# A linear-attention and tanh-shrink kernel on one core: the last tile's output in two transfers instead of four, and one middle tile's in four instead of two

## The chip, the cores and the metric

The kernel runs on one core of one Trainium2 chip. The metric is the device time of one execution in microseconds (us); lower is better. The core has five engines: TensorE (PE) for matrix products, VectorE (DVE), ScalarE (ACT), GpSimd (POOL) and SyncE (SP), which here only begins transfers. The transfers themselves are carried by the core's 16 DMA engines.

## The reference

`q`, `k` and `v` have the shape (8, 8, 576, 64): batch, heads, sequence, head size. The first part is linear attention with phi(x) = elu(x) + 1, the second a layer of two matrix products with x - tanh(x) between them.

```python
def phi(x):
    return np.where(x > 0, x, np.exp(x) - 1.0) + 1.0
q_p, k_p = (phi(q), phi(k))
kv = np.einsum('bhsd,bhse->bhde', k_p, v)
z = np.sum(k_p, axis=2)
num = np.einsum('bhsd,bhde->bhse', q_p, kv)
den = np.einsum('bhsd,bhd->bhs', q_p, z)[..., None] + 1e-06
attn_out = num / den
...
x = attn_out.transpose(0, 2, 1, 3).reshape(B * S, H * D)   # 4608 x 512
h = x @ w_in                                               # 512 -> 2048
g = h - np.tanh(h)
out = g @ w_out                                            # 2048 -> 512, float32
```

## The kernel before, in words

**Tiling.** The 4608 tokens are taken in nine chunks (`NC = 9`, loop over `c` at line 557) of 512. The attention of each of the eight batches is computed piecemeal between the matrix products of the chunks before it; its result lands transposed in `xT`. For a chunk, the first layer runs over 16 blocks of 128 hidden columns (line 654 on): four accumulating products (`l1mm`, line 413) a block, then ScalarE's tanh and VectorE's subtraction into `gT` (`l1act2`, line 417). The second layer (line 673 on) runs over four tiles `i` of 128 tokens, each a sum of 16 products of 128 x 512 (`l2mm`, line 433). The order of all work on the engines is the order in which the program is written; small tables (`s1`, `s2`) say after which block or step which piece of the next batches' attention is done.

**Tokens and rows.** Within a batch, a token is numbered s = 9 p + j, with p from 0 to 63 and j from 0 to 8 (`J = 9`). A chunk's columns are ordered by j first and p second, so a tile of 128 tokens is two groups of 64: partitions 0 to 63 hold one j, partitions 64 to 127 the next. Two neighbouring partitions of a group are nine output rows apart. The last tile of the program (chunk 8, tile 3) holds j = 7 and j = 8 of the last batch.

**How a tile leaves.** `evac` (line 438) is called once for a finished tile. It takes a new `osb` buffer (128 x 512 float32, one of five), copies the tile's columns `f0` to `f1` out of the accumulator, on ScalarE or, if `f0` is not 0, on VectorE, and begins the transfers to `out`. There is one transfer for each of the tile's two groups of 64 partitions (`half`), of 64 rows of 2048 bytes. In chunk 3, the transfers of tiles 0 and 1 are cut at column 256, so that there are four of 64 rows of 1024 bytes to a tile (`cuts`, line 449). All of these are begun by SyncE, with one exception below.

**The last tile** (line 678 on) is summed in two parts, columns 0 to 383 and then columns 384 to 511, with 16 products each, and `evac` is called for each part: first with `f0 = 0`, `f1 = 384`, copied by ScalarE, then with `f0 = 384`, `f1 = 512`, copied by VectorE. For this tile (`last`, line 446) the first group of 64 partitions is sent by SyncE and the second by ScalarE (line 451). After that only the program's closing is left: SyncE waits for the transfers that are still under way, and the engines meet at a barrier.

**Counts.** 78 transfers go to `out` in all: 66 of 128 KB, 8 of 64 KB, and, for the last tile, two of 96 KB and two of 32 KB.

Of the kernel before, what the change touches and what calls it, by code (L numbers as in the profile page):

```python
# [18 lines left out]
def kernel(  # L19
# [9 lines left out]
    nc = tc.nc  # L29
    B, H, S, D = q.shape  # L30
# [5 lines left out]
    NC = N // 512  # L36
    J = S // 64
# [400 lines left out]
    def evac(c, i, o, f0=0, f1=None):  # L438
        f1 = DM if f1 is None else f1
        osb = opool.tile([128, DM], F32, name="osb")  # L440
        if f0:
            nc.vector.tensor_copy(osb[:, f0:f1], o[:, f0:f1])  # L442
        else:
            nc.scalar.copy(osb[:, f0:f1], o[:, f0:f1])  # L444

        last = c == NC - 1 and i == 3
        for half in range(2):
            b, j = divmod(2 * (4 * c + i) + half, J)
            cuts = [f0, 256, f1] if c == 3 and 2 * i + half < 4 else [f0, f1]
            for a0, a1 in zip(cuts, cuts[1:]):  # L450
                (nc.scalar if last and half else nc.sync).dma_start(
                    out=out[b * S:(b + 1) * S, a0:a1].rearrange("(p j) m -> p j m", j=J)[:, j, :],
                    in_=osb[64 * half:64 * half + 64, a0:a1])

# [17 lines left out]
    for n in range(2):  # L472

        nc.gpsimd.dma_start(out=w_out_sb[:, 8 + 2 * n:10 + 2 * n, :],
                            in_=moe_w_out[1024 + 256 * n:1280 + 256 * n, :].rearrange("(ko ki) f -> ki ko f", ki=128))
# [3 lines left out]
    for h in range(2):  # L479
        for hg in range(2):  # L480
            for i in range(2):
                m = 4 * hg + 2 * h + i
# [74 lines left out]
    for c in range(NC):  # L557
# [44 lines left out]
        elif n1 < B:  # L602
# [11 lines left out]
            m = 12 if c == 1 else 9  # L614
# [58 lines left out]
        for s in range(16):  # L673

            (g, i) = divmod(s, 4) if c == 0 else (s % 4, s // 4)
            if g == 0:
                os_[i] = ps_all[:, i if c == 0 else 4 + i % 2, :]
            if c == NC - 1 and i == 3:

                if g == 0:  # L680
                    o2 = ps_all[:, 0, :]
                    for o, f in ((os_[i], slice(0, 384)), (o2, slice(384, DM))):
                        for fi in range(NF):
                            nc.tensor.matmul(o[:, f], gT[:, fi, 384:512], w_out_sb[:, fi, f],  # L684
                                             start=(fi == 0), stop=(fi == NF - 1))
                        evac(c, i, o, f.start, f.stop)
                continue
            if c == 0 and g == 2:
                for n in (2 * i, 2 * i + 1):
                    f = 8 + 2 * (n // 4)  # L690
                    l2mm(gT, os_[n % 4], n % 4, f, f + 2)
            else:
                l2mm(gT, os_[i], i, 4 * g, 4 * g + 4)
            if g == 3:
                evac(c, i, os_[i])
            for f in s2[s]:
                f()
# [30 lines left out]
```

## Time and profile before

| | |
|---|---|
| median of 3 runs | 286.83 us (286.57 to 286.95) |
| the profiled execution, its own time | 286.75 us |
| its span, first to last instruction | 285.0 us |
| mean granted TensorE clock | 0.997 |
| end of the last product (L684) | 280.84 us |
| ScalarE's copy of the last tile's 384 columns (L444) | 279.97, 0.48 us |
| VectorE's copy of its 128 columns (L442) | 280.86, 0.29 us |
| transfers to `out` begun by SyncE at L451 | 76, each 0.47 to 1.05 us of SyncE, median 0.59 |
| transfers to `out` begun by ScalarE at L451 | 2, of 0.56 and 0.68 us |

The span is the time from the first to the last instruction of the profiled execution; the difference to its own time lies ahead of and behind the program. Times within the profile count from the span's start. PE is TensorE, with PEld its weight loads; "SPq" and "ACTq" are the sequencers of SyncE and ScalarE, which issue transfers; "q1" and "q10" are the DMA queues of SyncE's and of ScalarE's transfers, "q0" that of GpSimd's. A transfer is made of packets, here one for each contiguous row, and of small packets of 4 bytes that tell of its completion. "us to landing" counts from the issue to the last of these. The DMA share of a window is the mean busy share of the 16 DMA engines; where packets of one engine overlap in the records it can exceed 1.

### The profile page before, as it was taken

To read this page: it belongs to the slowest core of one execution; us is meant where nothing else is said; L and a number is where in the kernel's file an instruction comes from. 1 tells how busy PE (TensorE), PEld (TensorE's weight loads), DVE (VectorE), ACT (ScalarE), POOL (GpSimd) and SP (SyncE) were. 2 spreads that over 40 slices of the span, in tenths; PEclk is the share of its full clock that TensorE was granted. 3 is DMA by queue.
4 is the path that set the end of the run, shared out by engine and by line. 5 is a ranking of instruction groups with operands and counts; after the bars stand their busy time and mean duration, and the time that the engine had idled before them with its cause. 6 is when DMAs were issued, how large, how long until landed. Compare 5 with 4: busy or idle time off the path is not lost.

```text
span 285.0 us, 5076 instructions
## 1 busy us (share of the span) xinstructions
PE 278.0 (98%) x2085; PEld 130.7 (46%) x2085; DVE 174.1 (61%) x271; ACT 147.4 (52%) x182; POOL 74.2 (26%) x66
## 2 busy tenths in 40 slices
PE   8989999999999999999999999999999999999994
PEld 3544454444444454445444544444444444444442
DVE  3759967997479773877397639764870166007500
ACT  4848557847345663666366635573642364135410
POOL 8642030030260536143604360506050000000000
PEclk9999999999999999999999999999999999999998
DMA  6999999998992399038903692232014200330033
GB/s 100 195 206 213 207 207 208 230 169 160 227 234 56 71 195 219 1 85 150 239 9 83 105 236 62 68 89 56 20 45 112 58 17 2 74 74 0 2 74 75
DMA packets 38215, 32.99 MB, mean 116 GB/s; under 512 B 16016, under 2 KB 33840, under 8 KB 38064
## 3 DMA queue, kind: packets, MB, share of 16 engines
q0 software_dynamic: 17488, 18.35, 39.7%
q1 hardware_dynamic: 20544, 14.18, 20.1%
q8 instruction: 16, 0.26, 0.4%
q10 hardware_dynamic: 160, 0.13, 0.2%
q14 instruction: 7, 0.06, 0.0%
HBM read 38.01 MB, written 9.46 MB: 167 GB/s over the span
## 4 chain that ended last, share of the span: by engine, by line
PE 85%; DMA 11%; POOL 2%; issue 0%; DVE 0%; POOLq 0%
PE ps_all L435 40%; PE ps_all L414 39%; DMA v<-in_v_dram 8%; DMA w_in_sb<-in_moe_w_in_dram 3%; PE ps_all L179 2%; PE ps_all L267 1%; PE ps_all L684 1%; POOL kraw L88 1%; POOL v L88 0%; POOL qraw L88 0%; POOL v L469 0%; PE ps_all L275 0%; POOL qraw L91 0%; PE ps_all L326 0%; PE ps_all L161 0%
## 5 line engine op out<-in xcount | busy, mean ns | idle before, releaser
L414 PE MATMUL ps_all<-xT,w_in_sb 128*128 128x512 bf16 x574 | 125.7, 379 | 0.0
L435 PE MATMUL ps_all<-w_out_sb,gT 128*128 128x512 bf16 x560 | 124.6, 379 | 0.0
L421 DVE TENSOR_TENSOR gT<-ps_all,th 128x1024 bf16<-128x1024 f32 x64 | 77.8, 1218 | 47.0 <-ACT th L420 47.0
L420 ACT ACTIVATE th<-ps_all 128x1024 f32<-128x1024 f32 x64 | 65.5, 1023 | 47.7 <-PE ps_all L414 47.7
L414 PEld LDWEIGHTS <-w_in_sb 128*128 128x128 bf16 x574 | 55.9, 98 | 67.3
L435 PEld LDWEIGHTS <-gT 128*128 128x128 bf16 x560 | 53.8, 98 | 63.3 <-issue 0.2
L444 ACT COPY osb<-ps_all 128x512 f32<-128x512 f32 (+1 forms) x36 | 20.8, 582 | 56.3 <-PE ps_all L435 40.0
L238 POOL TENSOR_TENSOR qp<-qp,rd 128x1152 bf16<-128x1152 bf16 x10 | 21.0, 2117 | 39.1 <-issue 23.6
L224 POOL TENSOR_TENSOR pr<-qp,zb 128x1152 f32<-128x1152 bf16 x10 | 23.5, 2361 | 24.0 <-ACT zb L217 21.6
L131 ACT ACTIVATE e<-qraw 128x1152 bf16<-128x1152 bf16 x16 | 18.5, 1160 | 8.9 <-DMA qraw<-in_q_dram 8.9
L229 DVE TENSOR_REDUCE dn<-pr 128x9 f32<-128x576 f32 x20 | 14.5, 746 | 12.2 <-POOL pr L224 12.2
L131 ACT ACTIVATE e<-kraw 128x1152 bf16<-128x1152 bf16 x15 | 17.4, 1162 | 0.1
L133 DVE TENSOR_TENSOR qp<-e,r 128x1152 bf16<-128x1152 bf16 x16 | 12.1, 759 | 5.5 <-ACT e L131 4.6
L133 DVE TENSOR_TENSOR kp<-e,r 128x1152 bf16<-128x1152 bf16 x15 | 11.4, 759 | 5.5 <-ACT e L131 4.6
L91 POOL DMA_DIRECT2D kraw<-in_k_dram x7 | 5.6, 803 | 28.1 <-ACT e L131 19.8
L426 DVE TENSOR_TENSOR gT<-ps_all,th 128x512 bf16<-128x512 f32 x16 | 10.3, 686 | 2.4 <-ACT th L425 1.7
L425 ACT ACTIVATE th<-ps_all 128x512 f32<-128x512 f32 x16 | 9.2, 598 | 4.6 <-PE ps_all L414 3.4
L91 POOL DMA_DIRECT2D qraw<-in_q_dram x7 | 5.2, 744 | 23.5 <-DVE r L132 13.0
L497 PE MATMUL ps_all<-zero 128*128 128x512 bf16 x29 | 9.5, 491 | 1.2 <-DVE zero L456 1.2
L374 DVE CAST xT<-ps_all 128x1024 bf16<-128x1024 f32 x5 | 6.1, 1217 | 6.9 <-PE ps_all L275 6.9
L132 DVE TENSOR_SCALAR r<-qraw 128x1152 bf16<-128x1152 bf16 x16 | 7.5, 467 | 3.2 <-DMA qraw<-in_q_dram 3.2
L442 DVE COPY osb<-ps_all 128x128 f32<-128x128 f32 x1 | 0.3, 292 | 11.6 <-PE ps_all L684 11.6
(96 smaller groups left out, 132.4 us busy)
## 6 DMA issues: line engine op xcount, KB each, us to landing
out_dram<-osb SPq DMA_DIRECT2D x66, 128.0 KB, 2.4
kraw<-in_k_dram POOLq DMA_DIRECT2D x7, 576.0 KB, 6.8
qraw<-in_q_dram POOLq DMA_DIRECT2D x7, 576.0 KB, 8.8
v<-in_v_dram POOLq DMA_DIRECT2D x7, 576.0 KB, 12.0
w_in_sb<-in_moe_w_in_dram POOLq DMA_DIRECT2D x3, 512.0 KB, 13.0
w_out_sb<-in_moe_w_out_dram POOLq DMA_DIRECT2D x3, 512.0 KB, 18.8
rdb<-ds SPq DMA_DIRECT2D x2, 576.0 KB, 7.9
qraw<-in_q_dram POOLq DMA_DIRECT2D x2, 288.0 KB, 4.5
```

Of the source, the lines that this page charges most:

```text
L91: nc.gpsimd.dma_start(out=t.rearrange("q h i j d -> q (h i) (j d)"), in_=x.rearrange("(n q) x -> q n x", n=4))
L131: return (lambda: nc.scalar.activation(e, x, AF.Exp), lambda: nc.vector.tensor_scalar(r, x, 0.0, 1.0, ALU.max, ALU.add), lambda: nc.vector ...
L133: lambda: nc.vector.tensor_tensor(y, e, r, ALU.min))
L224: nc.gpsimd.tensor_mul(pr_t[b][:, i].rearrange("p j h d -> p j (h d)"), qp_t[b][:, i].rearrange("p j h d -> p j (h d)"), zb_t[b][:, i].uns ...
L229: nc.vector.tensor_reduce(dn_t[b][:, i, :, h], pr_t[b][:, i, :, h, :], mybir.AxisListType.X, ALU.add)
L238: nc.gpsimd.tensor_mul(x, x, rd[:, i].unsqueeze(2).to_broadcast([128, J * 2, D]))
L414: nc.tensor.matmul(h, w_in_sb[:, p, fi * 128:(fi + 1) * 128], xT[:, p, c * 512:(c + 1) * 512], start=(n == 0), stop=(n == NP - 1))
L420: nc.scalar.activation(th, h, AF.Tanh)
L421: nc.vector.tensor_sub(gT[:, fi:fi + 2, :], h, th)
L426: nc.vector.tensor_sub(gT[:, fi, :], h, th)
L435: nc.tensor.matmul(o, gT[:, fi, i * 128:(i + 1) * 128], w_out_sb[:, fi, :], start=(fi == 0), stop=(fi == NF - 1))
L444: nc.scalar.copy(osb[:, f0:f1], o[:, f0:f1])
```

## The change

The last tile no longer goes through the loop over its two groups of 64 partitions. Each of the two calls of `evac` for it begins one transfer, from SyncE, of all 128 partitions: 128 rows of 1536 bytes (192 KB) for the first call and 128 rows of 512 bytes (64 KB) for the second. The destination is written as a pattern of three dimensions, j (2 values) by p (64) by columns; the source is the `osb` buffer's 128 partitions by columns. ScalarE begins no transfers any more.

In chunk 3, tile 2 is now cut at column 256 too: it leaves in four transfers of 64 rows of 1024 bytes instead of two of 2048. (The old condition `2 * i + half < 4` held for tiles 0 and 1.) The number of transfers to `out` stays 78.

```diff
-        last = c == NC - 1 and i == 3
+        if c == NC - 1 and i == 3:
+            nc.sync.dma_start(
+                out=out[(B - 1) * S:, f0:f1].rearrange("(p j) m -> j p m", j=J)[J - 2:J],
+                in_=osb[:, f0:f1])
+            return
         for half in range(2):
             b, j = divmod(2 * (4 * c + i) + half, J)
-            cuts = [f0, 256, f1] if c == 3 and 2 * i + half < 4 else [f0, f1]
+            cuts = [f0, 256, f1] if c == 3 and i < 3 else [f0, f1]
             for a0, a1 in zip(cuts, cuts[1:]):
-                (nc.scalar if last and half else nc.sync).dma_start(
+                nc.sync.dma_start(
                     out=out[b * S:(b + 1) * S, a0:a1].rearrange("(p j) m -> p j m", j=J)[:, j, :],
                     in_=osb[64 * half:64 * half + 64, a0:a1])
```

## The prediction

> **What bounds the kernel now.** I read the page first, then the chain of waits over the end of the span, then the end engine by engine, then the transfers there, since the diff touches only what follows the last results and one pair of transfers in the middle.
>
> ```profile
> span 285.0 us, 5076 instructions
> PE 278.0 (98%) x2085; PEld 130.7 (46%) x2085; DVE 174.1 (61%) x271; ACT 147.4 (52%) x182; POOL 74.2 (26%) x66
> ```
>
> TensorE is busy for 278.0 of 285.0 us, so the body is its own time, and a transfer counts only where TensorE waits for it or where nothing but the transfer is left. The chain of waits from 262 us on shows where the second begins:
>
> ```profile
> 266.97 10.36 PE ps_all L435 x48
> 277.33 3.51 PE ps_all L684 x32
> 280.84 0.02 issue
> 280.86 0.29 DVE osb L442
> ```
>
> The chain's last piece of work is VectorE's copy of 128 columns, done at 281.15. From there to 285.0 lie 3.85 us in which no engine computes: the output leaves and the program closes. Everything the diff does to the last tile falls here, in the open. The end in order of time:
>
> ```profile
> 279.97 0.48 ACT L444 COPY osb<-ps_all 128x384 f32<-128x384 f32 x1 [2.01 <-DMA out_dram<-osb]
> 280.48 1.18 SPq L451 DMA_DIRECT2D out_dram<-osb  x2
> 280.48 1.39 ACTq L451 DMA_DIRECT2D out_dram<-osb  x2
> ```
>
> ScalarE's copy of 384 columns ends at 280.45; SyncE and ScalarE then each begin a transfer of 64 rows of 1536 bytes at 280.48, and one of 64 rows of 512 bytes at about 281.19, as soon as the VectorE copy is done. What the DMA engines did meanwhile (columns: window, length, five engines, clock, DMA share, GB/s):
>
> ```profile
> 281.50:281.60 0.10, 0.00 (x0) 0.00 (x0) 0.00 (x0) 0.00 (x0) 0.00 (x0) 1.00 0.05 15
> ...
> 281.90:282.00 0.10, 0.00 (x0) 0.00 (x0) 0.00 (x0) 0.00 (x0) 0.00 (x0) 1.00 1.00 200
> ...
> 282.20:282.30 0.10, 0.00 (x0) 0.00 (x0) 0.00 (x0) 0.00 (x0) 0.00 (x0) 1.00 1.16 384
> ...
> 282.90:283.00 0.10, 0.00 (x0) 0.00 (x0) 0.00 (x0) 0.00 (x0) 0.00 (x0) 1.00 0.08 5
> ```
>
> First bytes move just before 281.6, 1.1 us after the issue; all 16 engines are full by 281.7; the bulk is over by 282.9 and a few late packets end at 283.2. The last landing is ScalarE's 32 KB transfer:
>
> ```profile
> out_dram<-osb SPq DMA_DIRECT2D x1, 96.0 KB, 2.1
> out_dram<-osb ACTq DMA_DIRECT2D x1, 32.0 KB, 2.8
> ```
>
> 281.19 + 2.8 = 284.0. From that landing to the span's end is 1.0 us of closing, which the change does not touch. The profiled execution took 286.75 us, so 1.75 us lie outside its span; it is 0.08 below the median of 286.83.
>
> **The change, part by part.**
>
> Mid transfers. The third tile of chunk 3 leaves in four transfers of 1024-byte rows instead of two of 2048. SyncE begins them at 136.08. Four issues at about 0.6 us (the issue row's median is 0.59) keep it until 138.5; its next transfer cannot begin before the next tile's copy is done:
>
> ```profile
> 139.03 0.59 ACT L444 COPY osb<-ps_all 128x512 f32<-128x512 f32 x1 [2.71 <-PE ps_all L435]
> ```
>
> That is 139.62, 1.1 us later, and behind it SyncE has nothing until the transpose at 153.2. The four run beside the loads for the coming chunk; the v load, issued at 133.22 with 10.1 us to landing, is there at 143.3, and no engine takes up that chunk's inputs before ScalarE's exponential at 153.77. Bytes stay the same. Cost taken: 0, hidden by those 10 us; without that cover it would be the two added issues, 1.2 us. Below nothing it can't go, since TensorE is full in every microsecond from 126 to 146.
>
> Removed at the end. ScalarE's two issues (0.56 and 0.68 us) and SyncE's two of 64 rows. ScalarE has no work behind them, so this frees nothing by itself.
>
> Added at the end. Two SyncE issues of 128 rows. Eight-row issues took 0.29 us, 64-row ones 0.47, so by the line through them 128 rows take 0.67: 280.48 to 281.15, just when the 128 columns are ready. If an issue took 1.0 us instead, the second would begin at 281.5, and its rows, as the next step shows, have to wait far longer than that anyway. Cost: 0.
>
> How many DMA engines carry them. Here lies the whole sum. The old destination was 64 rows by columns. The new one is written "j p m": its outermost count is 2 (the two row residues j), then 64, then the columns; the source stays 128 partitions. No transfer of this trace has an outermost count of 2. The nearest rows: the 32 KB and 96 KB transfers of ScalarE's queue (64 rows outermost), and four of 8 rows at 66.5 to 68.3 (L355), alone in their queue (first line: transfers by queue from 281.4 to 283.4; second: from 66.5 to 68.3; packets, MB, share):
>
> ```profile
> q10 hardware_dynamic: 160, 0.13, 22.0%
> ...
> q1 hardware_dynamic: 64, 0.02, 6.8%
> ```
>
> Of 160 packets, 128 are rows, leaving 32 completion packets of 4 bytes, 16 a transfer, which I read as one for each engine. Of 64, 32 are rows, leaving 32, so 8 a transfer: eight rows outermost, eight engines. Bounds: 2 engines, if the outermost count goes on setting it, and 16, if the 128 rows are shared out like the 64. An outermost count of 2 is nearer to 8 than to 64, so I take 2.
>
> The Trainium skill, page "DMA: Bandwidth & Descriptors", section "Why a DMA increments its semaphore by 16 and not by 1", states that the engines used are the largest number up to 16 that divides both sides' slowest dimension; 2 and 128 give 2. Its section "Rules for kernel authors" speaks for the change in one line (two transfers of partition halves only serialize, use one of 128 partitions) and against it in another (an outermost size below 16 confines the transfer to that many engines). The eight-row transfers here, on 8 engines, agree with the rule; a 2 beside a 128 no run here shows yet. By the rule the sum is that of 2 engines, by the line on partition halves alone it would be that of the 16-engine rival below.
>
> Time on 2 engines. Each carries 64 rows of 1536 bytes, then 64 of 512, one after the other, since both transfers stand in SyncE's queue. The packet records of the end give 65 ns (median in ScalarE's transfer) to 111 (in SyncE's, where 16 engines pulled at 64 partitions) for 1536 bytes, and 27 to 34 ns for 512. With two engines moving instead of 16 I expect less crowding, so I take 65 and, between 27 and 34, 30: 64 x 65 = 4.16 us, 64 x 30 = 1.92 us, together 6.1. As a cross-check, 384 GB/s over 16 engines is 24 GB/s each, and 131,072 bytes at that rate are 5.5 us. Lower bound: consecutive packets in that burst start 53 and 23 ns apart, 64 x 76 = 4.9 us. Upper: 111 and 34, 9.3 us.
>
> The sum: first bytes 281.6, + 6.1 = 287.7; + 0.4 from last packet to landing (SyncE's 96 KB: last packet at 282.2, landed at 282.6); + 1.0 closing = 289.1 us of span, where it was 285.0; + 1.75 = 290.8 us. Bounds: 289.6 with 4.9, 294.0 with 9.3. Where the stall goes: SyncE's closing waits stand on these two transfers, and nothing else is late.
>
> **The rivals.**
>
> *Sixteen engines all the same* (the other side). If the shape is shared out over 16 engines, eight rows each, the wide part moves as it does now, and the narrow part, begun at 281.19, ends at 282.9 without ScalarE's copy of the traffic; landed 283.3 instead of 284.0, it saves 0.7 us at best and nothing if the late packets up to 283.2 remain: 286.3 us. For it speaks that the 64-row transfers, the closest in size, post 16 completions; against it the 8-row ones. The deciding point: 128 rows over e engines at 65 + 30 ns are 12.2/e us, against 1.6 us now (281.6 to 283.2): from 8 engines up it is not slower.
>
> *Two engines, each packet paying its own latency.* In the records the last four 512-byte packets of the present run, following an 8 KB instruction fetch on one engine, start some 60 ns apart, though nothing else moves. At 60 for the narrow and 111 for the wide rows: 7.1 + 3.8 = 10.9 us, 295.6 us. Against it: narrow packets elsewhere in the same 2 us follow each other at 23 ns.
>
> *The mid transfers cost something.* It needs the loads late by more than 10 us; it would add at most 1.2 us to either case. I give it no chance of its own.
>
> **How the numbers follow.** Two engines at ordinary packet times: 0.83. Two engines, slower still: 0.08. Sixteen engines: 0.09, of which 0.06 is faster by over 0.2% (0.6 us, about what a measurement of this kernel can tell from no change) and 0.03 within it. Time: the likeliest case's 290.8 us. Range: that case's bounds, 289.6 to 294.0; what it leaves out is 0.17 plus a little noise. Faster 0.06, same 0.03, slower 0.91.
>
> **What would show it.** Right: the page's queue 10 is gone or empty; in the last stretch DMA share sits near 2/16 = 0.12 and about 45 GB/s for some 6 us; the 192 KB transfer takes 5 to 6 us from issue to landing and the 64 KB one 6 to 7; the chain up to VectorE's copy still ends near 281.15. The completion packets of the two transfers number 4, not 32. Wrong: share near 1 after 281.6 (16 engines), or a copy that ends later than 281.3, which would put the cost into the middle.

## The result and the profile after

The changed kernel takes 291.07 us (291.0 to 291.6, 5 runs) against 286.58 us (286.37 to 286.95, 5 runs) for the kernel before: a ratio of 1.0158, interval 1.0146 to 1.0171. It is 4.5 us slower. The forecast was 290.8 us, range 289.6 to 294.0.

The profiled execution is the slowest of the five, 291.6 us, with a span of 289.7. The chain of waits reaches VectorE's last copy almost as early as before, and SyncE begins both transfers without delay (chain of the span's end, then SyncE's timeline: start, length, what):

```profile
281.10 0.29 DVE osb L442
```

```profile
280.71 1.23 SPq L447 DMA_DIRECT2D out_dram<-osb  x2
```

The copy ends at 281.39 instead of 281.15: the body was 0.24 us longer in this execution, and the whole rest of the 4.7 us of span lies behind it. The same stretch that was 3.8 us long (281.15 to 285.0) is 8.3 us long (281.39 to 289.7). What the DMA engines do in it (window, length, five engines, clock, DMA share, GB/s):

```profile
281.90:284.50 2.60, 0.00 (x0) 0.00 (x0) 0.00 (x0) 0.00 (x0) 0.00 (x0) 0.83 0.14 33
284.50:286.90 2.40, 0.00 (x0) 0.00 (x0) 0.00 (x0) 0.00 (x0) 0.00 (x0) 0.50 0.13 50
286.90:288.40 1.50, 0.00 (x0) 0.00 (x0) 0.00 (x0) 0.00 (x0) 0.00 (x0) 0.50 0.14 43
288.40:289.70 1.30, 0.00 (x0) 0.00 (x0) 0.00 (x0) 0.00 (x0) 0.00 (x0) 0.50 0.00 0
```

A share of 0.13 to 0.14 of 16 engines is two engines, busy for 6.5 us, where before all 16 were full for one. 50 GB/s is 25 for each of the two in the wide rows, 43 is 21.5 in the narrow ones; the first 2.6 us bring only 33. The clock column falls to 0.50 only in this end, 2.6 us after TensorE's last product (281.06); up to there it is 1.0. The longer end at 0.50, not a slower body, makes the span's mean clock 0.990, where it was 0.997. The transfers by queue, over the same end:

```profile
q1 hardware_dynamic: 260, 0.26, 11.9%
```

260 packets are 256 rows and 4 completions, two for each transfer, where the old four transfers had 64. ScalarE's queue q10 is no longer in the page.

### The profile page after: what moved, and what is told of

Read it like the earlier page. It is cut to its first block, busy times and chain, and to the rows that moved or that the text cites. A ratio compares the mean times of both kernels' runs of the same rounds, so it can differ in the third digit from the quotient of the medians.

```text
span 289.7 us, 5047 instructions
## 1 busy us (share of the span) xinstructions
PE 275.7 (95%) x2057; PEld 130.9 (45%) x2085; DVE 174.1 (60%) x271; ACT 147.5 (51%) x182; POOL 74.1 (26%) x66
## 4 chain that ended last, share of the span: by engine, by line
PE 87%; DMA 5%; issue 1%; POOL 1%; DVE 1%; ACT 1%; SPq 0%; DVEq 0%; POOLq 0%
PE ps_all L414 43%; PE ps_all L435 39%; DMA v<-in_v_dram 3%; DMA out_dram<-osb 2%; PE ps_all L179 2%; PE ps_all L267 1%; ACT osb L444 1%; PE ps_all L290 1%; POOL kraw L88 0%; SPq L455 0%; DVE xT L294 0%; POOL qraw L88 0%; PE ps_all L326 0%; PE ps_all L161 0%; DVE rden L335 0%
## 5 line engine op out<-in xcount | busy, mean ns | idle before, releaser
L435 PE MATMUL ps_all<-w_out_sb,gT 128*128 128x512 bf16 x544 | 122.7, 379 | 1.3 <-issue 0.8
L420 ACT ACTIVATE th<-ps_all 128x1024 f32<-128x1024 f32 x64 | 65.6, 1024 | 47.9 <-PE ps_all L414 47.1
L374 ACT CAST xT<-ps_all 128x1024 bf16<-128x1024 f32 x5 | 5.1, 1012 | 4.3 <-PE ps_all L275 3.7
```

Of the source, the lines that this page charges most:

```text
L374: copy(xT[:, 2 * h:2 * h + 2, S * b:S * b + 512], ps_all[:, 2 * h:2 * h + 2, :])
L420: nc.scalar.activation(th, h, AF.Tanh)
L435: nc.tensor.matmul(o, gT[:, fi, i * 128:(i + 1) * 128], w_out_sb[:, fi, :], start=(fi == 0), stop=(fi == NF - 1))
```

## The experiments

The experiments are compared by their medians against runs of the kernel before on the same chip (286.74 to 286.93 us), and by their end stretch: from the end of VectorE's last copy to the end of the span, in the profiled execution. That stretch leaves out what the body varies by from one execution to the next.

| run | what | us | ratio, interval | end stretch |
|---|---|---|---|---|
| before | | 286.58 | | 3.8 |
| after | the change | 291.07 | 1.0158, 1.0146 to 1.0171 | 8.3 |
| e1 | middle part alone | 287.26 | 1.0014, 1.0005 to 1.0023 | 4.4 |
| e2 | last tile's part alone | 291.19 | 1.0148, 1.0131 to 1.0165 | 8.4 |
| e3 | outermost count 64 | 285.68 | 0.9955, 0.9941 to 0.9970 | 2.9 |
| e4 | wide part merged only | 290.53 | 1.0124, 1.0108 to 1.0140 | 7.3 |
| e5 | before + two small copies | 286.14 | 0.9983, 0.9974 to 0.9992 | 3.1 |
| e6 | before + 8 mid transfers | 286.73 | 1.0000, 0.9991 to 1.0009 | 4.0 |
| e7 | outermost count 16 | 286.81 | 1.0005, 0.9996 to 1.0014 | 3.9 |
| e8 | outermost count 4 | 289.36 | 1.0090, 1.0075 to 1.0106 | 6.3 |
| e9 | after + two small copies | 291.48 | 1.0160, 1.0145 to 1.0176 | 8.3 |
| e10 | narrow part merged only | 287.24 | 1.0013, 1.0004 to 1.0023 | 4.2 |
| e11 | after without narrow part | 289.79 | 1.0099, 1.0083 to 1.0115 | 6.7 |
| e12 | narrow part from ScalarE | 291.32 | 1.0155, 1.0138 to 1.0172 | 8.3 |

**The two halves of the change (e1, e2).** e1 is the kernel before with the new condition alone (its edit is shown); e2 is the changed kernel with the old condition put back, so that only the new block for the last tile is left.

```diff
-            cuts = [f0, 256, f1] if c == 3 and 2 * i + half < 4 else [f0, f1]
+            cuts = [f0, 256, f1] if c == 3 and i < 3 else [f0, f1]
```

> The change's middle part alone: chunk 3, tile 2 in four transfers, the last tile as before. Engine-count theory (all of the loss comes from the last tile's two transfers running on 2 DMA engines): no change, 286.6 us, ratio 1.000 within 0.002. Rival (the two added transfers in the middle delay later work): 0.5 to 4.5 us more, and the last product ends later than 281.2 in the profile.

> The change's last-tile part alone, chunk 3 as before. Engine-count theory: the whole loss, 291.0 us (290.7 to 291.4). Rival of the middle: less than that by what the middle costs.

e2 has the whole loss. e1 was expected at no change within 0.002; its ratio of 1.0014 lies inside that, but it is clear of 1 and worth 0.4 us. The profile says where it is not: VectorE's last copy begins at 280.97, 0.11 us later than in the kernel before, and the rest is behind it. There SyncE's closing waits give themselves away (the instructions of the closing line, first in e1 from 284.2 to 284.8, then in the kernel before from 283.9 to 284.2: times, ns, first and last start):

```profile
L723 SPq EVENT_SEMAPHORE  x8: 28/28/28, 284.3 to 284.7; - x8
```

```profile
L723 SPq EVENT_SEMAPHORE  x2: 28/28/28, 284.0 to 284.1; - x2
```

The closing goes through the eight transfer semaphores one by one in a fixed order, each about 62 ns after the one before when nothing has to be waited for: seven steps in 0.43 us in e1. With 78 transfers the last ones hold the last two places of that order, so that nearly all the waits are over when they land; with 80 they hold the first two, and six waits come after the last landing that did not before, 0.37 us. The end stretch is longer by another 0.16 us, because the last landing itself comes that much later behind the copy in this execution.

**Is it the place in the order, or the added transfers? (e6)**

```diff
-            cuts = [f0, 256, f1] if c == 3 and 2 * i + half < 4 else [f0, f1]
+            cuts = [f0, 256, f1] if c == 3 or c == 4 and i < 2 else [f0, f1]
```

> The kernel before with eight transfers more in the middle (all four tiles of chunk 3 and two of chunk 4 in four transfers each); the last tile as before. Transfers take eight semaphores in turn, and SyncE's closing waits go through them one by one, about 62 ns each, in a fixed order; with eight more the last transfers hold the same two as in the kernel before (the last of the order), with two more (e1) the first two. Theory (e1's 0.4 us is the six closing waits that come after the last landing): 286.8 us, ratio 1.000 within 0.001. Rival (e1's 0.4 us is the price of two added transfers in the middle): four times that, 288.4 us.

Eight more transfers in the middle, with the old places at the end, cost nothing: 1.0000. So the split transfers are free as work, and what e1 paid is mainly the order of the closing waits. In the changed kernel the last tile has two transfers fewer and the middle two more, 78 again, and the places are kept; in e2, with 76, two closing waits follow the last landing. That would be 0.12 us, which is the difference of the medians, but their runs overlap.

**One transfer for each part, on 16 engines (e3).** The last tile's tokens are reordered where batch 7's columns of `xT` are written, j inside and p outside, so that the destination can be walked with p (64) outermost, in the source's order. What is computed stays as it is; only the last tile's partitions stand in another order.

```diff
+                    y = x[:, :, 448:576].rearrange("q a (t j) -> q a t j", j=2)
+                    copy(x[:, :, 0:448], ps_all[:, 2 * h:2 * h + 2, 0:448])
+                    copy(y[:, :, :, 0], ps_all[:, 2 * h:2 * h + 2, 448:512])
+                    copy(y[:, :, :, 1], rest[h])
...
-                out=out[(B - 1) * S:, f0:f1].rearrange("(p j) m -> j p m", j=J)[J - 2:J],
+                out=out[(B - 1) * S:, f0:f1].rearrange("(p j) m -> p j m", j=J)[:, J - 2:J],
```

> The changed kernel, still one SyncE transfer of 128 rows for each part of the last tile and ScalarE sending nothing, but the last tile's tokens stand with p outermost and j inside, so that the destination's outermost count is 64 instead of 2 (two small copies more when batch 7's columns are written). Engine-count theory: 16 engines again, the loss is gone: 286.0 to 286.7 us, 16 completion packets for each of the two transfers. Rival (one transfer of 128 rows, or one queue alone, is what costs): about 291.0 us still.

285.68 us: 0.3 below the expected range, 1.1 below the kernel before and 5.4 below the changed one, with the same number of transfers from the same queue. Its end by queue, and in windows:

```profile
q1 hardware_dynamic: 288, 0.26, 27.8%
```

```profile
281.60:282.30 0.70, 0.00 (x0) 0.00 (x0) 0.00 (x0) 0.00 (x0) 0.00 (x0) 1.00 0.80 285
282.30:282.70 0.40, 0.00 (x0) 0.00 (x0) 0.00 (x0) 0.00 (x0) 0.00 (x0) 1.00 0.53 154
```

288 packets are 256 rows and 32 completions, 16 a transfer. 285 GB/s instead of 33 to 50, and all is moved in 1.0 us. Merging, or the single queue, was not the cost.

**What e3 gained over the kernel before (e5, e9).** In the kernel before, one 8 KB instruction fetch stands among the last packets, at 282.49 (transfers by queue from 281.5 to 283.3):

```profile
q14 instruction: 1, 0.01, 1.1%
```

In e3 it came at 269.4, and the end has no such line. e5 and e9 add e3's two small copies, in the old order, to the kernel before and to the changed one.

```diff
-                copy(xT[:, 2 * h:2 * h + 2, S * b:S * b + 512], ps_all[:, 2 * h:2 * h + 2, :])
+                n = 512 if b < B - 1 else 448
+                copy(xT[:, 2 * h:2 * h + 2, S * b:S * b + n], ps_all[:, 2 * h:2 * h + 2, 0:n])
+                if n < 512:
+                    copy(xT[:, 2 * h:2 * h + 2, S * b + n:S * b + 512], ps_all[:, 2 * h:2 * h + 2, n:512])
```

> The kernel before, with nothing of the change, and batch 7's columns written by the same two small copies more as in e3, here without any change of order. It tells apart two sources of e3's gain over the kernel before. In e3 the 8 KB instruction fetch that stood at 282.5 us, among the last packets, stood at 269.4. Theory A (most of e3's 1.1 us is that fetch, gone from the open end): 286.0 to 286.3 us, with the fetch near 269 and the last landing near 283.3. Theory B (the gain is the merged transfers on 16 engines): 286.7 us as before, whether the fetch moves or not.

> The changed kernel plus the two small copies of e5, with no change of order: the control for e3, whose destination shape and two copies changed together. Engine-count theory: the copies are not what e3 gained its 5.4 us from; 290.6 to 291.4 us. Rival (the instruction fetch that the copies move makes a good part of the changed kernel's loss): below 290.4.

In both, the fetch moved away from the end, to 269.9 in e5 (transfers by queue from 269 to 271) and to 269.2 in e9:

```profile
q14 instruction: 1, 0.01, 1.6%
```

e5 gained 0.6 us against its own runs of before (286.14 against 286.74). That is the time that theory A gave, and not the 286.7 of theory B; but it is only about half of e3's 1.1, so the merged transfers have a part too. Its last landing is at 283.6 with the copy 0.4 later than in the kernel before. The packet records show two things that the fetch delayed: the last row ends 0.3 us sooner behind the copy without it, and from that row to the last landing pass 0.35 us instead of 0.82. By the end stretches, 3.8, 3.1 and 2.9 (one execution each), the fetch out of the way is worth 0.7 us and the merged transfers on 16 engines 0.2; by the medians, 286.14 and 285.68 with intervals of the ratio that don't overlap, the second is 0.5. Between 0.2 and 0.5 it stays open. e9 shows that the fetch had no part in the loss: 291.48 with the fetch gone from the end, 0.1 above the range expected and far from the rival's 290.4.

**Other outermost counts (e7, e8).** The edit is e8's; e7 has `a=16` and `0:8` in its place. In both, the last tile's rows go to other rows of the output.

```diff
-                out=out[(B - 1) * S:, f0:f1].rearrange("(p j) m -> j p m", j=J)[J - 2:J],
+                out=out[N - 256:, f0:f1].rearrange("(a r) m -> a r m", a=4)[:, 0:32],
```

> The changed kernel with the destination's outermost count set to 16 (16 groups of 8 neighbouring rows; the last tile's rows go to other places of the output, same number and size of rows). Engine-count theory: 16 engines, 16 completion packets a transfer, about 0.9 us of data instead of 6.5: 285.5 to 286.4 us. Rival (a merged transfer, or the single queue, costs whatever the shape): 291 us.

> The same with an outermost count of 4 (4 groups of 32 neighbouring rows; the last tile's rows go to other places of the output). Engine-count theory: 4 engines, 32 rows each of 61 and 24 ns, 2.7 us of data, up to 3.7 with the gaps that the changed kernel's profile shows at the start: 287.3 to 288.4 us, 4 completion packets a transfer. Rival: as for 16 groups.

Both came out above the expected times by 0.4 and 1.0 us. 0.6 us of that is an effect of the experiment: their rows are also written by earlier tiles, and SyncE waits for those transfers (four wait instructions at the two transfers' line, where the changed kernel has two), so that the wide transfer begins 0.6 us after ScalarE's copy instead of at once. For e7 that settles it; for e8 0.4 stays open. Its packets and its speed:

```profile
q1 hardware_dynamic: 264, 0.26, 14.3%
```

```profile
282.30:284.10 1.80, 0.00 (x0) 0.00 (x0) 0.00 (x0) 0.00 (x0) 0.00 (x0) 1.00 0.24 48
284.10:285.00 0.90, 0.00 (x0) 0.00 (x0) 0.00 (x0) 0.00 (x0) 0.00 (x0) 1.00 0.27 101
```

264 packets less 256 rows are 8 completions, 4 a transfer; 101 GB/s is again 25 for each of four engines, once the slow beginning is over. Counts of 2, 4, 16 (e7) and 64 (e3) thus give 2, 4, 16 and 16 engines, and 6.5, 3.9, 1.4 and 1.0 us from the first packet to the last.

**The two terms apart (e4, e10, e11).** e4 and e10 make the new block's condition hold for one part alone, the other going in halves from SyncE and ScalarE; e11 leaves the narrow transfer out. Of the edits one line is shown, e10's; e4 has `and not f0` there. e10 also has one middle transfer fewer in halves than the change, which makes 78 in all.

```diff
-        if c == NC - 1 and i == 3:
+        if c == NC - 1 and i == 3 and f0:
...
```

> Only the 384-column part goes as one transfer with outermost count 2; the 128-column part goes in halves from SyncE and ScalarE as before. Engine-count theory: the narrow rows are spread over 16 engines, and only those that fall to the two busy ones wait behind the wide rows (8 of them each at 24 ns); the end moves up by the narrow part's 1.5 us less 0.2: 289.5 to 290.0 us. Rival (the loss goes with the number of merged transfers, half for each): about 288.8 us.

> Only the 128-column part goes as one transfer with outermost count 2; the 384-column part goes in halves from SyncE and ScalarE; one mid transfer more in halves, so that the last transfers keep their place in the closing waits. Engine-count theory: the wide rows are gone by 282.5, then 64 rows of 24 ns on 2 engines end at 284.0: 287.1 to 287.4 us; 288.4 if the gaps of 1.1 us that the wide transfer showed at its start come with every transfer on 2 engines. Rival (each merged transfer costs the same): 288.9.

> The changed kernel with the 128-column transfer left out (these columns of the last tile are not written). Engine-count theory: the narrow part's 1.5 us go: 289.5 us. It also tells where the changed kernel's gaps of 1.1 us among the first wide packets come from: if from the second transfer being issued beside the first, they go too, 288.4 us.

e10 is as the engine count has it: the narrow rows alone, after the wide ones on 16 engines, cost 0.3 us against their runs of before. Its end in windows:

```profile
281.60:282.60 1.00, 0.00 (x0) 0.00 (x0) 0.00 (x0) 0.00 (x0) 0.00 (x0) 1.00 0.76 205
282.60:284.20 1.60, 0.00 (x0) 0.00 (x0) 0.00 (x0) 0.00 (x0) 0.00 (x0) 1.00 0.14 41
```

Two engines move the 64 KB in 1.6 us, without the slow beginning. e11, at 289.79, is 0.3 above the 289.5 that the missing narrow rows gave and far above the 288.4 without the gaps. e4, at 290.53, missed its 289.5 to 290.0; it has 79 transfers, the one that lands last holds the first place in the closing waits, and seven of them, 0.43 us, follow that landing at 287.04. Without them it would stand at 290.1, still 0.1 too high.

**The other queue (e12).**

```diff
-            nc.sync.dma_start(
+            (nc.scalar if f0 else nc.sync).dma_start(
```

> The changed kernel with the 128-column transfer begun by ScalarE, so on the other queue. If both queues put a transfer of outermost count 2 on the same two engines: 291.0 us, the two kinds of packets now mixed. If the second queue takes other engines: the narrow rows run beside the wide ones, 289.5 us.

291.32 us, and each queue shows 130 packets, 128 rows and 2 completions. Its end in windows:

```profile
281.60:285.40 3.80, 0.00 (x0) 0.00 (x0) 0.00 (x0) 0.00 (x0) 0.00 (x0) 0.82 0.14 39
285.40:287.00 1.60, 0.00 (x0) 0.00 (x0) 0.00 (x0) 0.00 (x0) 0.00 (x0) 0.50 0.14 48
287.00:288.10 1.10, 0.00 (x0) 0.00 (x0) 0.00 (x0) 0.00 (x0) 0.00 (x0) 0.50 0.14 42
```

The DMA share stays 0.14 all along, so in none of the three were four engines at work: the second queue brought no second pair. The middle window is the one that tells, since there both kinds of rows move: the wide rows now start 85 ns apart, which is their own 61 and a narrow row's 24, so the two queues took turns on the same two engines. Before that the packets were not mixed: the narrow rows began only at 285.5, although ScalarE's issue was over at 282.2. Why they waited is not shown.

## Why the prediction was right

**What bounds, and where it lies.** Right: e2 alone has the whole loss, and it is all behind VectorE's copy. One sign that the prediction had named for being wrong did come, a copy that ends later than 281.3 (281.39), which was to put the cost into the middle. It does not: that end moves from one execution to the next, from 280.72 in e2, which has the whole loss, and 280.85 in e9, which has both parts of the change, to 281.52 in e5, which has neither. Of the signs for being right, the two landing times were a little too short: by the closing waits the 192 KB took 6.5 us from the issue (5 to 6 expected) and the 64 KB 7.3 (6 to 7).

**Two engines, by the outermost count.** This was the step that held the sum, and it was taken from one row, eight rows on eight engines. It is shown by the 4 completions, the DMA share of 0.13, and the series 2, 4, 16 of e2, e8 and e7. The divisor rule of the Trainium skill, page "DMA: Bandwidth & Descriptors", section "Why a DMA increments its semaphore by 16 and not by 1", agrees with all of them, counts of 64 beside 128 included (16 engines in e3). Its advice against two transfers of partition halves, in "Rules for kernel authors", is worth the 0.2 to 0.5 us between e5 and e3 here, and only where the outermost count stays large.

**The sizes.** Wide part: 4.16 us predicted, 5.0 measured (281.93 to 286.93). The packets follow each other at 61 ns, a little faster than the 65 taken, but gaps among the first two dozen of each engine add 1.1 us that the sum did not have. Narrow part: 1.92 predicted, 1.5 measured, at 23.6 ns instead of 30. Together 6.5 instead of 6.1. The lower bound's 53 ns between wide packets did not come: at 61 and 23.6 ns without any gap the two engines need 5.4 us, not 4.9. First packet at 281.9 instead of 281.6 (0.24 of it the later copy), last packet to landing 0.3 instead of 0.4, closing 0.9 instead of 1.0. These make a span of 289.7 where the sum had 289.1. The other four executions had spans of 289.1 to 289.3; only against them, and so against the median, is the time right to 0.3 us. That closeness is partly luck: misses that cancel. The two issues took 0.59 and 0.52 us, not 0.67, and cost nothing, as expected.

**Middle transfers at nothing.** Right as work (e6), but the reason was half of it: the predicted cover of 10 us says nothing on which places the last transfers get in the closing waits. Alone, this part costs 0.4 us (e1).

**The rivals.** Sixteen engines all the same: did not come, and where the shape allows 16 engines (e3) its price was too high: 286.3 us against 285.7 measured, a gain of 1.1 us where it had 0.7 at best. The late packets that it left open are those behind the instruction fetch, about 0.6 us of that gain (e5). The deciding point of 8 engines was not tried. Each packet paying its own latency: fell; 61 and 23.6 ns throughout the second half.

## What to carry to other kernels

Before two transfers are merged into one, look at the outermost count on both sides: a count of 2 put 256 KB on 2 of 16 DMA engines and cost 4.5 us where nothing could hide it, while the same merge with 64 outermost gained 0.2 to 0.5 us. Count the small completion packets in the profile to see how many engines a transfer had. And at the end of a program, see what else stands in the open stretch: the order of the closing waits (0.4 us) and an instruction fetch among the last packets (about 0.6 us) were each worth about as much as that gain or more.

## What had not been expected of the hardware

- A transfer that falls on two or four idle engines starts unevenly. In the changed kernel the packets of both engines stop together, at the same offsets in the kernel after, e2 and e9 (stops of 190 to 320 ns within the first 2.5 us, 1.1 us in all), and run evenly after. It is neither the second transfer (e11 loses 0.9 us in the same way) nor the instruction fetch (e9). The narrow rows, which in the changed kernel and in e10 began right behind other rows, had none. A slow beginning does not need few engines, though: in the kernel before and in e7, on 16 engines, three in four of the wide rows of the first 0.5 us took over 95 ns each, where in e3 none took more than 80. The cause stays open.
- One 8 KB instruction fetch of 0.3 to 0.6 us on a DMA engine holds back the rows that the engine has still to move, and with rows spread over all engines the output waits for it (3.8 against 3.1 us of end stretch, before and e5). More than half of that difference lies behind the last row, between it and the last landing (0.82 against 0.35 us); why is not shown.
- From the issue's start to the first packet pass 1.1 us on SyncE's queue with 64 wide rows (before, e10) and 1.2 to 1.3 with 128 (the kernel after, e2, e3).
